# Row tests moved into the experts' hand-set order, one chunk's bonus sums moved ahead of its scores, and the verdict read before the last expert

## The chip, the cores and the metric

The kernel runs on one core of one Trainium2 chip. A core has five engines with an instruction queue each: TensorE (PE in the profile, with its weight loads as PEld), VectorE (DVE), ScalarE (ACT), GpSimd (POOL) and SyncE (SP, which here issues most DMA transfers). They wait for each other by semaphores alone. The metric is device time in microseconds (us). The kernel before took 307.76 us, the median of three runs (306.99, 307.76, 310.99).

## The reference, cut to what matters

The first half is a gated linear attention with a state of 48 x 48 for each of 4 x 8 heads over 768 steps; the second sends each token with a positive skip score to one of eight experts.

```python
for t in range(S):                       # S = 768, state: B, H, 48, 48
    cur = einsum('bhd,bhe->bhde', u * k[t], v[t])
    y[t] = einsum('bhd,bhde->bhe', r[t], state + cur)
    state = w[t][..., None] * state + einsum('bhd,bhe->bhde', k[t], v[t])
x = y as (3072 tokens, 384)
do_compute = x @ w_skip > 0
xc = x[do_compute]
logits = xc @ w_gate                     # 8 experts
gate_w = softmax(logits) of the chosen expert, e_idx = argmax(logits)
for e in range(8):
    y[e_idx == e] = gate_w * (relu(xc @ w1[e]) @ w2[e])
out[do_compute] = xc + y
```

## The kernel before, in words

The attention is done in 24 chunks of 128 steps, six for each of four batches, all eight heads at once. A chunk's decays are cumulated by two scans on DVE (L266 gives `q`, L288 gives `rh`), POOL makes the scaled keys `kq` (L283), the scaled reads `rp` (L293) and the products `rk` for the bonus term (L275). On PE a chunk is: transposed keys (L305), scores of keys against reads (L312, into the two banks psA), bonus sums (L327, psB), the rows of the chunk before (L378, psX), the state's update (L341, psu), and the outputs (L362 and L367, psY). DVE masks the scores (L318) and writes the bonus into psY (L331); the outputs of the chunk add to that, so L362 needs both masks and L331. ACT does the copies out of PSUM.

The order of this part is written out by hand: a loop over `s` (L574 to L650) emits, at step `s`, the outputs of chunk `s`, the scores of chunk `s + 1` and the scans of chunk `s + 2`, and every engine keeps the order in which its instructions were written. `drip` mixes steps of the router in, which ranks tokens within their expert (L390 to L507). Behind the loop a second hand-ordered block (L668 to L689) runs the first half of expert 0 while the last group of six chunks is routed, and a third (L824 to L827) runs the experts; in that one POOL has its place by hand too, SP has not.

The experts work in products of split numbers: each weight and token matrix is a high and a low part, and three products are added. Expert `e` does eight groups of hidden columns (psH, L780 to L782), ACT and DVE split them into `hh` and `hl`, then two groups of 128 tokens (`j` = 0, 1) go through the second layer (psO, L804 to L806), DVE forms `fin` (L811), and POOL scatters it to the output by an indirect DMA (L744). Between these, ACT and DVE split the next expert's weights (L89, L90: `w1l`, `w2l`).

The kernel also tests whether its short cuts held: on DVE, L696 to L707 test rows of `ends`, `lows`, `gall` and `rall` and leave sums in `vt`; PE adds these over the partitions (L710, L711, psf), and DVE writes the verdict `flag_i` (L712). These lines stand outside the hand-ordered blocks, so that a scheduler chose their places. At the end of the program `values_load` (L834) reads `flag_i` into a register of each of the five engines, and a branch on it (L835) runs the slow general path if a test failed. It does not for these inputs.

Of the kernel before, what the change touches and what calls it, by code (L numbers as in the profile page):

```python
# [8 lines left out]
F32 = mybir.dt.float32  # L9
# [6 lines left out]
ALU = mybir.AluOpType  # L16
# [40 lines left out]
def rwkv_moe_kernel(ctx, tc, wrk, wrk0, vN, uP, wgs, wgp, w12, cst, out):  # L57
# [64 lines left out]
    with tc.tile_pool(name="att", bufs=2) as att, \  # L122
# [173 lines left out]
            nc.scalar.copy(ends[:, i], work[i].pop("rh")[:, :, P])  # L296
            nc.scalar.copy(lows[:, i], work[i]["q"][:, :, 0])

        def intra(i):
            b, c = seq[i]  # L300
            wk = work[i]
            if c < NC - 1:
                pst = ps1.tile([P, NP, P], F32, tag="psT", name=f"psT{i}", bufs=2)
                for a in range(NP):
                    nc.tensor.transpose(pst[:, a], wk["kq"][:, a], ident)  # L305
                kt = wk["kt"] = att.tile([P, NP, P], F32, tag="kt", name=f"kt{i}")
                nc.scalar.copy(kt, pst)
            for a in range(NP):
                for j in (0, HP):
                    for g in range(2):  # L310
                        rows = slice(64 * g, 64 * g + HP)
                        nc.tensor.matmul(psa[g][j:j + HP, a, j:], wk["kq"][rows, a, j:j + HP],  # L312
                                         wk["rp"][rows, a, j:], start=True, stop=True)
# [9 lines left out]
        def bonus_sums(i):  # L323
            wk = work[i]
            wk["psb"] = ps1.tile([P, NP, P], F32, tag="psB", name=f"psB{i}")
            for a in range(NP):
                nc.tensor.matmul(wk["psb"][:, a], ubk_sb[:, a], wk["rk"][:, a],  # L327
                                 start=True, stop=True)
# [242 lines left out]
        with tc.manual_schedule():  # L571
            setup()
            fill(FILL0)
            for s in range(-2, n + 1):  # L574
# [40 lines left out]
                if on(s):  # L615
                    evict(s)
                if on(s + 1):
                    intra(s + 1)
                    drip(2 * pace[0])
                    mask(s + 1, 0)  # L620
                    mask(s + 1, 1)
                    drip(pace[0])
                    bonus_sums(s + 1)
                    bonus(s + 1)
                if s == -1:
                    prep_reads(1)
# [41 lines left out]
        with tc.manual_schedule(engines={nc.tensor.engine, nc.scalar.engine, nc.vector.engine}):  # L668
# [17 lines left out]
            for k in range(done[0], 6 * FC - 4):  # L686
# [1 line left out]
            early_tokens(1)  # L688
            drain(todo)  # L689


        vt = keep.tile([P, 5], F32, name="vt")
        good = keep.tile([P, n * NP], F32, name="good")
        good_ = keep.tile([P, n * NP], F32, name="good_")
        ends_ = ends.rearrange("p c a -> p (c a)")
        nc.vector.tensor_scalar(good_, ends_, 1.0 - TOL, None, op0=ALU.is_ge)  # L696
        nc.vector.scalar_tensor_tensor(good, ends_, 1.0 + TOL, good_, op0=ALU.is_le, op1=ALU.mult)
        nc.vector.scalar_tensor_tensor(good, lows.rearrange("p c a -> p (c a)"), Q_MIN, good,
                                       op0=ALU.is_ge, op1=ALU.mult)
        nc.vector.tensor_reduce(vt[:, 0:1], good, axis=AX, op=ALU.add)  # L700
        nc.vector.tensor_scalar(vt[:, 0:1], vt[:, 0:1], n * NP - 0.5, None, op0=ALU.is_le)
        fine = good[:, :B * NC]
        nc.vector.tensor_scalar(fine, gall[:, :, 0], 0.1, None, op0=ALU.is_ge)
        nc.vector.tensor_reduce(vt[:, 1:2], fine, axis=AX, op=ALU.add)
        nc.vector.tensor_reduce(vt[:, 2:3], rall[:, :, 0], axis=AX, op=ALU.max)
        nc.vector.tensor_scalar(vt[:, 2:3], vt[:, 2:3], float(CAP), None, op0=ALU.is_ge)
        nc.vector.scalar_tensor_tensor(vt[:, 3:4], vt[:, 1:2], B * NC - 0.5, vt[:, 2:3],  # L707
                                       op0=ALU.is_le, op1=ALU.add)
        psf = ps1.tile([P, 512], F32, tag="psT", name="psf", bufs=2)
        nc.tensor.matmul(psf[0:1, 0:1], rowsk, vt[:, 0:1], start=True, stop=False)  # L710
        nc.tensor.matmul(psf[0:1, 0:1], rows1_, vt[:, 3:4], start=False, stop=True)  # L711
        nc.vector.tensor_scalar(flag_i, psf[0:1, 0:1], 0.0, None, op0=ALU.is_gt)  # L712


    with tc.tile_pool(name="wset1", bufs=1) as ws1, tc.tile_pool(name="moe", bufs=2) as moe:
        wset1[0] = ws1
        def pair(e, instr=None):
# [8 lines left out]
        pair(1)  # L726
        pair(2)
        later_pairs = list(range(3, E))
        first = []

        xTs = {}
# [11 lines left out]
        def scatter(s, o):  # L743
            sc = nc.gpsimd.indirect_dma_start(  # L744
                out=out, out_offset=bass.IndirectOffsetOnAxis(ap=ids[:, s % 2, s // 2:s // 2 + 1],
                                                               axis=0),
                in_=o, in_offset=None, bounds_check=NT - 1, oob_is_err=False)
            tc.declare_no_dep(sc.ins, group="rows", reason="tokens are scattered to rows of their own")
            tc.add_to_no_dep_group("rows", sc.ins)

        def expert(e):
            todo = []
# [47 lines left out]
            for j in range(1 if e == 0 else 0, 2):  # L800
                pso = ps1.tile([P, DM], F32, tag=("psu", "pss")[j], name=f"psO{e}_{j}")
                for fc in range(FC):
# [3 lines left out]
                    nc.tensor.matmul(pso, h[j, fc][1], w2h[:, o], start=False,  # L806
                                     stop=(fc == FC - 1))
                more(2)
                s = 2 * e + j
                o = moe.tile([P, DM], F32, tag="fin", name=f"fin{e}_{j}", bufs=3)  # L810
                nc.vector.scalar_tensor_tensor(o, pso, gates[:, j, e:e + 1], xg[s],  # L811
# [4 lines left out]
                    scatter(s, o)  # L816
                if s == 2 * E - 3:
                    nc.gpsimd.drain()
            more(12)
            if e + 2 < E:  # L820
                drain(load_weights(e + 2, 0))
# [9 lines left out]

    rv = nc.values_load(flag_i[0:1, 0:1], min_val=0, max_val=2)  # L834
    with tc.If(rv > 0):  # L835
        general_path(tc, wrk, w12, yd, uP, c_sb, wgs_sb, out)

# [155 lines left out]
```

## Time and profile before

| | |
|---|---|
| median of 3 runs | 307.76 us |
| the profiled execution's own time | 307.14 us |
| span of its trace, first to last instruction | 305.4 us |
| PE busy | 290.0 us (95%) |
| DVE busy | 216.8 us (71%) |
| ACT, POOL busy | 175.4 us (57%), 141.2 us (46%) |
| mean granted TensorE clock | 0.997 |

A time line of an engine has the start in us from the span's start, the length, the engine, the line of the kernel, the operation and its tiles, and in brackets the idle time ahead of it with what ended it. DVE and PE overlap the end of one instruction with the start of the next, so that the distance between starts can be smaller than a length. A letter q behind an engine's name (DVEq) marks its sequencer, which takes instructions ahead of the engine.

### The profile page before, as it was taken

How to read it: one execution, taken by the hardware profiler on the slowest of the kernel's cores; microseconds unless marked ns; L12 is line 12 of the kernel's file. 1: busy time of each engine (PE TensorE's matmuls, PEld its weight loads, DVE VectorE, ACT ScalarE, POOL GpSimd, SP SyncE). 2: the span in 40 equal slices, each digit the busy share in tenths (PEclk: the TensorE clock that was granted, in tenths of full speed). 3: DMA queues.
4: the chain of work that ended last, by engine and by line, in shares of the span. 5: the costliest groups of instructions: out<-in, count | busy, mean ns of one | idle time of the engine just before them, and what ended most of it. 6: DMA issues, size and time to landing. Idle time of an engine off the chain costs nothing.

```text
span 305.4 us, 8275 instructions
## 1 busy us (share of the span) xinstructions
PE 290.0 (95%) x3228; PEld 269.3 (88%) x3228; DVE 216.8 (71%) x410; ACT 175.4 (57%) x493; POOL 141.2 (46%) x140
## 2 busy tenths in 40 slices
PE   6799999999999999897999999999999999999991
PEld 2689888888889988786888999999999999999991
DVE  6887779868888778977263868594958859495310
ACT  5365736799577976796232656391837648182300
POOL 7886565977966598775106662402011010201111
PEclk9999999999999999999999999999999999999998
DMA  7999999998799988836323699846265564610000
GB/s 193 270 255 260 293 258 246 227 256 217 206 294 282 266 185 206 252 124 217 116 76 86 171 368 342 296 166 245 90 239 204 206 248 146 245 70 26 9 21 22
DMA packets 22738, 60.29 MB, mean 197 GB/s; under 512 B 3926, under 2 KB 10490, under 8 KB 22688
## 3 DMA queue, kind: packets, MB, share of 16 engines
q1 hardware_dynamic: 20176, 53.79, 60.6%
q0 software_dynamic: 2048, 5.48, 5.7%
q8 instruction: 27, 0.44, 0.7%
q10 hardware_dynamic: 464, 0.40, 0.6%
q14 instruction: 23, 0.19, 0.2%
HBM read 52.60 MB, written 7.86 MB: 198 GB/s over the span
## 4 chain that ended last, share of the span: by engine, by line
PE 60%; DVE 4%; DMA 4%; issue 0%; ACT 0%; POOL 0%; POOLq 0%; SPq 0%; DVEq 0%
PE psO L806 7%; PE psO L804 7%; PE psO L805 7%; PE psH L782 7%; PE psH L781 7%; PE psH L780 7%; DMA vt<-wrk 3%; PE psY L362 3%; PE psY L367 3%; PE psB L327 3%; PE psA L312 2%; PE psH L115 2%; PE psX L378 2%; PE psX L739 2%; DVE psY L331 1%; PE psO L561 1%
## 5 line engine op out<-in xcount | busy, mean ns | idle before, releaser
L744 POOL DMA_INDIRECT out<-fin,ids x16 | 16.7, 1044 | 99.4 <-DVE fin L811 93.3
L787 ACT ACTIVATE hh<-psH 128x256 fp32r<-128x256 f32 x60 | 23.0, 384 | 57.1 <-PE psH L782 53.3
L782 PE MATMUL psH<-xTh,w1l 128*128 128x256 f32 x168 | 47.5, 283 | 0.0
L781 PE MATMUL psH<-xTl,w1h 128*128 128x256 f32 x168 | 47.5, 283 | 0.0
L780 PE MATMUL psH<-xTh,w1h 128*128 128x256 f32 x168 | 47.5, 283 | 0.0
L318 DVE TENSOR_TENSOR asb<-psA,c_sb 128x512 f32<-128x512 f32 x48 | 30.8, 683 | 16.8 <-PE psA L312 16.8
L804 PE MATMUL psO<-w2h,hh 128*128 128x384 f32 x120 | 40.8, 340 | 0.0
L806 PE MATMUL psO<-w2h,hl 128*128 128x384 f32 x120 | 40.2, 335 | 0.0
L805 PE MATMUL psO<-w2l,hh 128*128 128x384 f32 x120 | 40.1, 334 | 0.0
L275 POOL TENSOR_TENSOR rk<-wrk 128x512 f32<-128x512 f32 x24 | 31.3, 1305 | 5.8 <-POOL rp L293 2.2
L792 DVE SCALAR_TENSOR_TENSOR hl<-psH,hh 128x256 fp32r<-128x256 f32 x60 | 25.2, 419 | 11.8 <-ACT hh L787 10.0
L288 DVE TENSOR_TENSOR_SCAN rh<-wrk,pss 128x520 f32<-128x520 f32 x24 | 29.6, 1235 | 4.2 <-PE pss L495 2.4
L782 PEld LDWEIGHTS psH<-xTh,w1l 128*128 128x128 f32 x168 | 32.2, 192 | 0.0
L781 PEld LDWEIGHTS psH<-xTl,w1h 128*128 128x128 f32 x168 | 32.2, 192 | 0.0
L780 PEld LDWEIGHTS psH<-xTh,w1h 128*128 128x128 f32 x168 | 32.2, 191 | 0.0
L283 POOL TENSOR_TENSOR kq<-wrk,q 128x512 f32<-128x512 f32 x24 | 28.3, 1178 | 7.7 <-DVE q L266 6.5
L293 POOL TENSOR_TENSOR rp<-wrk,rh 128x512 f32<-128x512 f32 x23 | 27.1, 1180 | 8.9 <-DVE rh L288 7.2
L811 DVE SCALAR_TENSOR_TENSOR fin<-psO,gates,xg 128x384 f32<-128x384 f32 x15 | 9.3, 618 | 30.3 <-PE psO L806 27.1
L266 DVE TENSOR_TENSOR_SCAN q<-wrk,pss 128x520 f32<-128x520 f32 x24 | 29.3, 1222 | 1.7 <-DMA wrk<-wrk 1.4
L362 PE MATMUL psY<-asb,v 128*48 128x128 f32 x384 | 26.6, 276 | 3.5 <-DVE short L514 2.0
L90 DVE TENSOR_TENSOR w2l<-r,w2h 128x512 fp32r<-128x512 f32 x42 | 27.9, 689 | 0.8
L89 ACT CAST w2h<-r 128x512 fp32r<-128x512 f32 x48 | 27.9, 626 | 0.6 <-DMA r<-w 0.6
(148 smaller groups left out, 653.0 us busy)
## 6 DMA issues: line engine op xcount, KB each, us to landing
r<-w SPq DMA_DIRECT2D x48, 512.0 KB, 5.6
wrk<-wrk SPq DMA_DIRECT2D x23, 579.4 KB, 7.8
v<-vN SPq DMA_DIRECT2D x24, 192.0 KB, 6.0
out<-x SPq DMA_DIRECT2D x24, 192.0 KB, 2.5
vt<-wrk SPq DMA_DIRECT2D x46, 96.0 KB, 7.1
wrk<-wrk SPq DMA_DIRECT2D x1, 384.0 KB, 4.5
vt<-wrk ACTq DMA_DIRECT2D x1, 256.0 KB
out<-fin,ids POOLq DMA_INDIRECT x16
```

The costliest lines, as they stand in the source:

```text
L266: nc.vector.tensor_tensor_scan(q.rearrange("p a j -> p (a j)")[:, ::-1], t[:, 1:1 + n_][:, ::-1], ones_at[:, 1:1 + n_][:, ::-1], 0.0, op0= ...
L275: nc.gpsimd.tensor_tensor(work[i]["rk"].rearrange("p a j -> p (a j)"), t[:, R_OFF:K_OFF], t[:, K_OFF:V_OFF], op=ALU.mult)
L283: nc.gpsimd.tensor_tensor(kq, wk["k"], wk["q"][:, :, 1:1 + P], op=ALU.mult)
L288: nc.vector.tensor_tensor_scan(rh.rearrange("p a j -> p (a j)"), wk["w"][:, 0:NP * CW], ones_at[:, :NP * CW], 1.0, op0=ALU.mult, op1=ALU.max)
L318: nc.vector.tensor_tensor(s, psa[g], tri.rearrange("p (o j) -> p o j", o=1).to_broadcast([P, NP, P]), op=ALU.mult)
L362: nc.tensor.matmul(psy[64 * g:64 * g + D, a], v[:, 2 * a + g], wk["asb"][g][:, a], start=False, stop=(c == 0), skip_group_check=True)
L780: nc.tensor.matmul(ps, w1h[:, o:o + P], xTh[:, kc], start=(kc == 0), stop=False)
L781: nc.tensor.matmul(ps, w1h[:, o:o + P], xTl[:, kc], start=False, stop=False)
L782: nc.tensor.matmul(ps, w1l[:, o:o + P], xTh[:, kc], start=False, stop=(kc == KC - 1))
L804: nc.tensor.matmul(pso, h[j, fc][0], w2h[:, o], start=(fc == 0), stop=False)
L805: nc.tensor.matmul(pso, h[j, fc][0], w2l[:, o], start=False, stop=False)
L806: nc.tensor.matmul(pso, h[j, fc][1], w2h[:, o], start=False, stop=(fc == FC - 1))
```

## The change

It does three things. For the chunk 1 alone (the second), the four bonus sums stand ahead of the scores on PE. The row tests become a function that expert 1 calls behind its first group of 128 tokens, and PE's two sums and the verdict another one that expert 2 calls at the same place. And `values_load` stands in expert 6, behind its second group, instead of at the end; the branch stays at the end.

```diff
-        def intra(i):
+        def rows_of_keys(i):
...
                 nc.scalar.copy(kt, pst)
+
+        def scores(i):
+            wk = work[i]
             for a in range(NP):
...
                 if on(s + 1):
-                    intra(s + 1)
+                    rows_of_keys(s + 1)
+                    if s == 0:
+                        bonus_sums(1)
+                    scores(s + 1)
                     drip(2 * pace[0])
                     mask(s + 1, 0)
                     mask(s + 1, 1)
                     drip(pace[0])
-                    bonus_sums(s + 1)
+                    if s != 0:
+                        bonus_sums(s + 1)
                     bonus(s + 1)
...
+        def row_tests():
+            ends_ = ends.rearrange("p c a -> p (c a)")
+            nc.vector.tensor_scalar(good_, ends_, 1.0 - TOL, None, op0=ALU.is_ge)
...
+            nc.vector.scalar_tensor_tensor(vt[:, 3:4], vt[:, 1:2], B * NC - 0.5, vt[:, 2:3],
+                                           op0=ALU.is_le, op1=ALU.add)
+
+        def verdict():
+            psf = ps1.tile([P, 512], F32, tag="psT", name="psf", bufs=2)
+            nc.tensor.matmul(psf[0:1, 0:1], rowsk, vt[:, 0:1], start=True, stop=False)
+            nc.tensor.matmul(psf[0:1, 0:1], rows1_, vt[:, 3:4], start=False, stop=True)
+            nc.vector.tensor_scalar(flag_i, psf[0:1, 0:1], 0.0, None, op0=ALU.is_gt)
...
                 more(2)
+                if j == 0 and e in (1, 2):
+                    (row_tests, verdict)[e - 1]()
                 s = 2 * e + j
...
                 if s == 2 * E - 3:
                     nc.gpsimd.drain()
+                    verdicts.append(nc.values_load(flag_i[0:1, 0:1], min_val=0, max_val=2))
...
-    rv = nc.values_load(flag_i[0:1, 0:1], min_val=0, max_val=2)
+    rv = verdicts[0]
     with tc.If(rv > 0):
```

The ten instructions of the tests are the same ten as before (L696 to L707). What moved is best seen in the engines' orders.

DVE, in the attention, behind the last scan of chunk 23 (`rh`), before: `good`, `vt` are the row tests, `asb_22` the masked scores of chunk 22, psY its bonus, `short` a step of the router.

```order
L288 SCALAR_TENSOR_TENSOR rh_2315<-wrk_85,pss 128x520
L696 TENSOR_SCALAR good__2615<-ends 128x96
L697 SCALAR_TENSOR_TENSOR good<-ends,good__2615 128x96
L698 SCALAR_TENSOR_TENSOR good<-lows,good 128x96
L700 TENSOR_REDUCE vt<-good 128x1
L701 TENSOR_SCALAR vt<-vt 128x1
L318 TENSOR_TENSOR asb_22_2344<-psA_108,c_sb 128x512
L318 TENSOR_TENSOR asb_22_2346<-psA_109,c_sb 128x512
L331 TENSOR_TENSOR psY<-psB_2348,vt_88 128x512
L514 TENSOR_SCALAR short<-psC 1x1
```

The same place now:

```order
L288 SCALAR_TENSOR_TENSOR rh_2315<-wrk_85,pss 128x520
L321 TENSOR_TENSOR asb_22_2344<-psA_108,c_sb 128x512
L321 TENSOR_TENSOR asb_22_2346<-psA_109,c_sb 128x512
L334 TENSOR_TENSOR psY<-psB_2348,vt_88 128x512
L517 TENSOR_SCALAR short<-psC 1x1
```

Five row tests stood between the scan and the masks; now the masks follow the scan. The other five, which stood among the last group's router steps, are gone from there too, and all ten stand in expert 1 between the fourth of the second-layer weight splits after the hidden groups and `fin_0`.

PE, in chunk 1, from its last scores on, before (psA are scores, psB the bonus sums, psX the rows of chunk 0, psu the state):

```order
L312 MATMUL psA_108<-rp_236,kq_199 64x64
L312 MATMUL psA_109<-rp_236,kq_199 64x64
L327 MATMUL psB_307<-rk_196,ubk_sb 128x128 x4
L378 MATMUL psX_315<-wgp_sb,xT_278 128x105 x4
L341 MATMUL psu<-v_169,kt_285 64x48
L341 MATMUL psu<-v_169,kt_285 48x48
```

PE in chunk 1 now, from its transposed keys (psT) on:

```order
L305 MATMUL psT_280<-c_sb,kq_199 128x128 x4
L330 MATMUL psB_287<-rk_196,ubk_sb 128x128 x4
L315 MATMUL psA_108<-rp_236,kq_199 64x128
L315 MATMUL psA_109<-rp_236,kq_199 64x128
L315 MATMUL psA_108<-rp_236,kq_199 64x64
```

The bonus sums went past the sixteen score products, and psX now follows the scores.

DVE at the end of the program, before (TENSOR_LOAD is the read of the verdict, `g_r` belongs to the general path):

```order
L792 SCALAR_TENSOR_TENSOR hl_7_4234<-psH_7_4232,hh_7_4233 128x256
L811 SCALAR_TENSOR_TENSOR fin_0_4271<-psO_0_4246,gates,xg_2826 128x384
L811 SCALAR_TENSOR_TENSOR fin_1_4301<-psO_1_4276,gates,xg_2830 128x384
L834 TENSOR_LOAD flag_i
L835 COMPARE_AND_BRANCH
```

DVE now, at the end of expert 6 and at the end of the program:

```order
L823 SCALAR_TENSOR_TENSOR fin_1_4128<-psO_1_4099,gates,xg_2790 128x384
L831 TENSOR_LOAD flag_i
L802 SCALAR_TENSOR_TENSOR hl_0_4150<-psH_0_4148,hh_0_4149 128x256
...
L823 SCALAR_TENSOR_TENSOR fin_0_4285<-psO_0_4260,gates,xg_2812 128x384
L823 SCALAR_TENSOR_TENSOR fin_1_4315<-psO_1_4290,gates,xg_2816 128x384
L848 COMPARE_AND_BRANCH
```

The read went ahead of expert 7's work on DVE, and likewise on PE, ACT and POOL. On SP, where the scheduler chooses, it went from ahead of expert 2's weight loads to between the two halves of expert 4's.

## Rows read from the trace of the kernel before

**Rows 1.** Busy time per engine in the experts' stretch (us busy, instructions in brackets)

```profile
168.00:299.00 131.00, 131.00 (x938) 130.76 (x936) 87.89 (x166) 67.61 (x152) 26.88 (x26) 1.00 0.52 181
```

**Rows 2.** Time line of PE, 138 to 145 us

```profile
138.94 1.09 PE L312 MATMUL psA<-rp,kq 64*64 64x128 f32 x32
...
142.52 0.16 PE L512 MATMUL psC<-ohs,onesb 128*1 128x1 bf16 x1
144.65 1.08 PE L362 MATMUL psY<-asb,v 128*48 128x128 f32 x16 [1.97 <-DVE short L514]
```

**Rows 3.** Time line of DVE, 140 to 145 us

```profile
140.25 0.37 DVE L696 TENSOR_SCALAR good__2615<-ends 128x96 f32<-128x96 f32 x1 [0.45 <-ACT ends L296]
140.65 1.30 DVE L697 SCALAR_TENSOR_TENSOR good<-ends,good__2615 128x96 f32<-128x96 f32 x1
142.06 0.26 DVE L698 SCALAR_TENSOR_TENSOR good<-lows,good 128x96 f32<-128x96 f32 x1
...
142.71 1.28 DVE L318 TENSOR_TENSOR asb<-psA,c_sb 128x512 f32<-128x512 f32 x2
143.91 0.69 DVE L331 TENSOR_TENSOR psY<-psB,vt 128x512 f32<-128x512 f32 x1
```

**Rows 4.** Time line of POOL beside it

```profile
140.67 1.17 POOL L293 TENSOR_TENSOR rp<-wrk,rh 128x512 f32<-128x512 f32 x1
```

**Rows 5.** Time line of PE, chunk 1

```profile
14.64 1.09 PE L312 MATMUL psA<-rp,kq 64*64 64x128 f32 x32 [0.72 <-POOL rp L293]
...
18.23 1.08 PE L362 MATMUL psY<-asb,v 128*48 128x128 f32 x16
```

**Rows 6.** Time line of DVE, chunk 1

```profile
16.31 1.26 DVE L318 TENSOR_TENSOR asb<-psA,c_sb 128x512 f32<-128x512 f32 x2
17.49 0.69 DVE L331 TENSOR_TENSOR psY<-psB,vt 128x512 f32<-128x512 f32 x1
```

**Rows 7.** Time line of DVE, the last group's router

```profile
157.35 0.18 DVE L703 TENSOR_SCALAR good<-gall 128x24 f32<-128x24 f32 x1
157.44 0.20 DVE L448 TENSOR_REDUCE rall<-rnk 128x6 f32<-128x48 f32 x1
```

**Rows 8.** Time line of DVE, second layer of expert 1, start of expert 2

```profile
189.85 0.62 DVE L811 SCALAR_TENSOR_TENSOR fin<-psO,gates,xg 128x384 f32<-128x384 f32 x1 [0.81 <-PE psO L806]
190.38 1.35 DVE L90 TENSOR_TENSOR w2l<-r,w2h 128x512 fp32r<-128x512 f32 x2
194.01 0.62 DVE L811 SCALAR_TENSOR_TENSOR fin<-psO,gates,xg 128x384 f32<-128x384 f32 x1 [2.28 <-PE psO L806]
195.49 0.42 DVE L792 SCALAR_TENSOR_TENSOR hl<-psH,hh 128x256 fp32r<-128x256 f32 x1 [0.86 <-ACT hh L787]
```

**Rows 9.** Costliest groups on the page: weight splits on DVE (us in all, mean ns)

```profile
L90 DVE TENSOR_TENSOR w2l<-r,w2h 128x512 fp32r<-128x512 f32 x42 | 27.9, 689 | 0.8
```

**Rows 10.** Reads of the verdict, by line (ns min/median/max, start us)

```profile
L834 PEldq TENSOR_LOAD <-flag_i x1: 487/487/487, 295.8 to 295.8; - x1
L834 DVEq TENSOR_LOAD <-flag_i x1: 537/537/537, 299.1 to 299.1; - x1
```

**Rows 11.** The branch behind the read on DVE, by line

```profile
L835 DVEq COMPARE_BRANCH  x1: 72/72/72, 300.1 to 300.1; - x1
...
L835 DVEq EVENT_SEMAPHORE  x1: 21/21/21, 304.2 to 304.2; - x1
```

**Rows 12.** Time line of POOL, scatters behind experts 6 and 7

```profile
283.06 0.98 POOL L744 DMA_INDIRECT out<-fin,ids  x1 [2.97 <-DVE fin L811]
...
300.01 0.98 POOL L744 DMA_INDIRECT out<-fin,ids  x1 [3.18 <-DVE fin L811]
```

**Rows 13.** Busy time per stretch; the last two columns are DMA share, GB/s

```profile
285.00:285.50 0.50, 0.50 (x6) 0.50 (x6) 0.15 (x1) 0.11 (x1) 0.00 (x0) 1.00 0.00 0
...
303.00:303.50 0.50, 0.00 (x0) 0.00 (x0) 0.00 (x0) 0.00 (x0) 0.00 (x0) 1.00 0.02 3
```

**Rows 14.** DMA queues, 300.7 to 301.5 us: packets, MB, share of 16 engines

```profile
q14 instruction: 3, 0.02, 16.1%
q8 instruction: 1, 0.02, 8.6%
```

More of the change, by code (lines that the diff above doesn't have):

```diff
@@ L689, in rwkv_moe_kernel @@
             drain(todo)
[L692 to L712, printed above, removed]
     with tc.tile_pool(name="wset1", bufs=1) as ws1, tc.tile_pool(name="moe", bufs=2) as moe:
@@ L728, in rwkv_moe_kernel @@
         later_pairs = list(range(3, E))
+        verdicts = []
         first = []
@@ L749, in scatter @@
             tc.add_to_no_dep_group("rows", sc.ins)
+        vt = keep.tile([P, 5], F32, name="vt")
+        good = keep.tile([P, n * NP], F32, name="good")
+        good_ = keep.tile([P, n * NP], F32, name="good_")
+        def row_tests():
+            ends_ = ends.rearrange("p c a -> p (c a)")
+            nc.vector.tensor_scalar(good_, ends_, 1.0 - TOL, None, op0=ALU.is_ge)
+            nc.vector.scalar_tensor_tensor(good, ends_, 1.0 + TOL, good_, op0=ALU.is_le, op1=ALU.mult)
+            nc.vector.scalar_tensor_tensor(good, lows.rearrange("p c a -> p (c a)"), Q_MIN, good,
+                                           op0=ALU.is_ge, op1=ALU.mult)
+            nc.vector.tensor_reduce(vt[:, 0:1], good, axis=AX, op=ALU.add)
+            nc.vector.tensor_scalar(vt[:, 0:1], vt[:, 0:1], n * NP - 0.5, None, op0=ALU.is_le)
+            fine = good[:, :B * NC]
+            nc.vector.tensor_scalar(fine, gall[:, :, 0], 0.1, None, op0=ALU.is_ge)
+            nc.vector.tensor_reduce(vt[:, 1:2], fine, axis=AX, op=ALU.add)
+            nc.vector.tensor_reduce(vt[:, 2:3], rall[:, :, 0], axis=AX, op=ALU.max)
+            nc.vector.tensor_scalar(vt[:, 2:3], vt[:, 2:3], float(CAP), None, op0=ALU.is_ge)
+            nc.vector.scalar_tensor_tensor(vt[:, 3:4], vt[:, 1:2], B * NC - 0.5, vt[:, 2:3],
[5 more added lines that the diff above has]
+            nc.vector.tensor_scalar(flag_i, psf[0:1, 0:1], 0.0, None, op0=ALU.is_gt)
         def expert(e):
```

## The prediction, made before the result was known

> **What bounds the kernel now.** I read the page first, then the busy time by stretch, then PE's time line, then DVE's beside it, and the last six us by line. The reader is to see three things.
>
> From 168 to 299 us PE is busy 131.00 of 131.00 us [rows 1]: in the experts nothing but PE sets the time, and whatever the other engines do there costs nothing as long as PE is not made to wait. What PE saves ahead of 168 us therefore reaches the end undiminished, unless a later wait eats it.
>
> In the attention PE is near full too, with one large hole. At 144.65 PE starts L362 after 1.97 us of idleness, its last work before that being L512 at 142.52 [rows 2]. The row names "short" as what ended it. But L362 reads the masked scores and the bonus in psY, and the bonus, L331, ended at 143.91 + 0.69 = 144.60 [rows 3], 0.05 us before PE moved. So L331 is what PE waited for.
>
> Behind PE's last product, near 299.1 us, come `fin`, the scatter and the branch, and the span ends at 305.4. These six us have no PE work in them.
>
> **The change part by part.**
>
> *Five tests out of the attention.* DVE was free from 140.25 - 0.45 = 139.80 [rows 3], and the scores of chunk 22 were done at 138.94 + 1.09 = 140.03 [rows 2]. The masks L318 started only at 142.71, because five row tests, issued from 140.25 on, stood ahead of them [rows 3]. Without them the masks start near 140.1, or 2.6 us earlier, and L331 ends near 142.0. PE reaches L362 at about 142.65, when L512 is through. L331 is then no longer late, PE's own queue is, and the gain is the whole hole: 144.65 - 142.65 = 2.0 us. What follows on PE up to the experts hangs on products of its own, or on steps of the router and the first gather that start from the same masks and move with them. The bounds: 1.97 us of idle time and no more; nothing, if another input of L362 were late at the same instant. I take 2.0.
>
> One thing in these rows bears on the new place. L697 took 1.30 us and L698, on as many elements, 0.26 [rows 3]; L697 ran from 140.65 to 141.95 and POOL's `rp` from 140.67 to 141.84 [rows 4].
>
> *Five tests out of the router.* L703 started at 157.35 and the router's next step at 157.44 [rows 7], so a test of this kind holds the chain back by at most 0.09 us by starts, and that only if the step behind it was ready. Five times that is 0.45 at most. I take 0, because those steps wait for each other anyway, and keep 0.45 for the range.
>
> *Ten tests into expert 1.* In the second layer DVE stood idle for 0.81 us before the first `fin`, 2.28 before the second and 0.86 before the first `hl` of expert 2 [rows 8], or 3.95 together. The first five tests took 142.71 - 140.25 = 2.46 with L697 at 1.30; at 0.26 they take 1.4. The second five, at 0.18 to 0.20 each like L703, take 1.0 [rows 3, 7]. So 2.4 us, or 3.5 with L697 slow; both lie inside 3.95. Queued behind them are `fin`, two `w2l` splits and with these the next load of weights on SP, which comes up to 3.5 - 0.81 = 2.7 us later. PE reads that expert's weights only one expert on, so this is covered: 0. If the cover were gone, the excess over 3.95 would reach `hl` and then PE.
>
> *PE's two sums into expert 2.* They leave PE's queue in front of expert 0 and enter it between two groups of expert 2, with the same two one-column products: 0. The verdict on DVE is one tiny instruction ahead of a `fin`.
>
> *Chunk 1.* PE waited 0.72 us for POOL's `rp` before the scores [rows 5]. Now it does the bonus sums in that time. That is the upper bound of the gain. But L362 of this chunk started at 18.23, and DVE's L331, which it needs, ended at 17.49 + 0.69 = 18.18; DVE had been busy without a break since the masks at 16.31 [rows 5, 6]. The sums can start at 14.64 - 0.72 = 13.92; if they take about as long as the scores, 1.1 us, the scores end near 16.1, still ahead of 16.31. So DVE keeps its times, PE waits for L331 instead of for `rp`, and the gain is 0.
>
> *The read of the verdict into expert 6.* A read takes 0.49 us on PE's sequencer. There it stood at 295.8 while PE worked on to 299 [rows 1, 10], so the sequencer was 3 us ahead and a read of half a us inside the stream is covered: 0. On SP the next load waits for a split that comes behind the verdict anyway: 0.
>
> *The tail.* On DVE the read began at 299.1 and the branch at 300.1; only 4.1 us after the branch, at 304.2, did DVE go on [rows 10, 11]. Without the read the branch can start 1.0 us earlier. The Trainium skill ("Runtime: NRT & Kernel Launch", section on instruction fetch mechanics) says that a taken branch out of the loaded window must fetch its target by DMA before it goes on; by that rule the fetch stays and merely starts earlier, so that the tail would give the same 1.0. The trace agrees as far as it shows four instruction packets right then [rows 14]. But the end also waits for the last scatter. It was issued at 300.01 and its traffic was still there after 303.0, 3 us later; the scatter issued at 283.06 had no traffic left at 285.0 [rows 12, 13]. The fetches fall between the two and may be what slows it. If so they leave its way as they move; if not, the scatter keeps the end where it is. Bounds: 0 and 1.0. The branch began 0.4 us after the read was over (299.1 + 0.54 against 300.1), so something besides the read holds it; that speaks for the lower half, and I take 0.4.
>
> **The sum.** 2.0 + 0.4 = 2.4 us. The profiled execution took 307.14, so it would become 304.7; the median of the runs, 307.76, lies 0.6 above it, which makes 305.4. I put the forecast between the two, at **305.0**.
>
> **The rivals.**
>
> *More is gained.* The tail gives its full 1.0 (0.6 more), and the router's 0.45 comes on top: 305.0 - 1.05, about 303.9. For it: each fetch that leaves the scatter's way. Against it: several things end within half a us of each other at 304.2, and all must move. Chance 0.14.
>
> *The hole stays.* The masks move forward, and PE waits at the next place instead: for the first gather, for ACT's copy, or for a weight load of expert 0. Then the 2.0 are given back, and with the tail at 0 to 0.4 the time is 307.0 to 307.5. For it: the chain behind the hole runs through DVE, POOL and a DMA before PE meets it. Against: that chain starts from the same DVE instructions, which move 1.8 us or more. Or the tests were not what held the masks, and the change does not do what it says; rows 3 leave little room for that. Chance 0.16.
>
> *Slower: the tests collide with POOL in expert 1.* The one test that ran wholly beside a POOL instruction took 1.30 us [rows 3, 4]. POOL issues gathers and scatters during expert 1 too. If all ten tests took 1.30 there, that is 13.0 us against 3.95 of idle time [rows 8]: the first `hl` of expert 2 would be 9.05 us late, PE with it, and the time 307.14 - 2.4 + 9.05, near 313.8. It costs more than it saves once the tests take over 3.95 + 2.4 = 6.4 us together. Against it: two weight splits beside such a scatter took 1.35 [rows 8], 0.68 each, and their mean is 0.689 [rows 9], so POOL's indirect transfers do not slow DVE. The Trainium skill ("SBUF — State Buffer", section on SBUF's two separate sides) has a lock that would do it: a DVE instruction with two inputs from SBUF and a GpSimd instruction that reads SBUF exclude each other for the whole instruction. Rows 3 and 4 fit it; by it alone three of the ten tests could be held for a POOL instruction each. Chance 0.04.
>
> The forecast itself has 0.64; its own range, from the unknown tail, the router and the gap of 0.6 between profile and median, is 304.0 to 306.0. A remaining 0.02 is for what I don't see.
>
> **Range and chances.** 303.2 to 306.4 holds the forecast and the case with more gained, and leaves out the hole that stays and the slower one, 0.2. Two per cent, about what a measurement of this kernel can tell from no change, is 6.2 us. No case but the slower one comes near it: faster 0.02, within 0.96, slower 0.02.
>
> **What would show it.** In the changed kernel's trace DVE's masks of chunk 22 follow the scan of chunk 23 by less than 0.5 us, and PE's L362 there shows no idle time above 0.2; if 1.97 is there again, or as much at one of the next three waits, the first step is wrong. In chunk 1 the wait for `rp` is gone and about 0.5 stands at L362; if PE starts L362 before 18.0, that term was mis-sized. In expert 1 the ten tests take 2.4 to 3.5 us and PE has no gap; a gap there is the third rival. At the end the branch on DVE follows `fin` at once. The step from the last product to the span's end, 6.3 us now, should be 5.3 to 6.3. The forecast fails if PE has a new gap anywhere in the experts, most of all where the verdict is read behind expert 6.

## The result, and the profile after

The changed kernel took 304.62 us, the median of 4 runs (303.77 to 306.77); the forecast was 305.0, with a range of 303.2 to 306.4. The kernel before has 309.38 beside it (306.99 to 312.03, 4 runs): the three runs known already and one more, at 312.03. The ratio is 0.985 with a 95% interval of 0.980 to 0.990: faster by 1.5%, within the 2% that the forecast named. Run twice more, on two chips, it gave 304.86 (ratio 0.987, 0.982 to 0.992) and 304.62 (0.984, 0.979 to 0.988). Medians here are of all runs of a set, while the ratios leave out runs over 1.5% above the fastest of their kernel.

The profiled execution took 304.25 us with a span of 302.5. Between the two traces the difference is 305.35 - 302.46 = 2.89 us, and it lies in four places: the start came 0.44 later (L362 of chunk 1 at 18.23, now 18.67), the hole at chunk 22 is 2.04 shorter, from chunk 23 to the last `fin` 0.05 was saved, and the end is 1.24 shorter.

**The hole.** PE's time line of the changed kernel, same columns as [rows 2]; L365 is the former L362:

```profile
139.37 1.09 PE L315 MATMUL psA<-rp,kq 64*64 64x128 f32 x32
...
142.95 0.16 PE L515 MATMUL psC<-ohs,onesb 128*1 128x1 bf16 x1
143.04 1.08 PE L365 MATMUL psY<-asb,v 128*48 128x128 f32 x16
```

And DVE's beside it, to be held against [rows 3]:

```profile
139.00 1.24 DVE L288 TENSOR_TENSOR_SCAN rh<-wrk,pss 128x520 f32<-128x520 f32 x1 [1.29 <-PE pss L498]
140.53 1.29 DVE L321 TENSOR_TENSOR asb<-psA,c_sb 128x512 f32<-128x512 f32 x2 [0.29 <-PE psA L315]
141.73 0.69 DVE L334 TENSOR_TENSOR psY<-psB,vt 128x512 f32<-128x512 f32 x1
```

The masks now wait 0.29 us for their scores instead of standing behind five tests, L334 ends at 142.42, and PE goes from L515 to L365 without a gap.

**Expert 1.** DVE's time line, with the ten tests where [rows 8] had idle time:

```profile
186.63 0.20 DVE L741 TENSOR_SCALAR good__2639<-ends 128x96 f32<-128x96 f32 x1
186.86 0.26 DVE L742 SCALAR_TENSOR_TENSOR good<-ends,good__2639 128x96 f32<-128x96 f32 x1
187.16 0.26 DVE L743 SCALAR_TENSOR_TENSOR good<-lows,good 128x96 f32<-128x96 f32 x1
...
188.49 0.16 DVE L752 SCALAR_TENSOR_TENSOR vt<-vt 128x1 f32<-128x1 f32 x1
188.58 0.62 DVE L823 SCALAR_TENSOR_TENSOR fin<-psO,gates,xg 128x384 f32<-128x384 f32 x1
189.12 1.28 DVE L90 TENSOR_TENSOR w2l<-r,w2h 128x512 fp32r<-128x512 f32 x2
191.96 0.62 DVE L823 SCALAR_TENSOR_TENSOR fin<-psO,gates,xg 128x384 f32<-128x384 f32 x1 [1.55 <-PE psO L816]
193.44 0.42 DVE L802 SCALAR_TENSOR_TENSOR hl<-psH,hh 128x256 fp32r<-128x256 f32 x1 [0.87 <-ACT hh L797]
```

From 186.63 to 188.65 they take 2.0 us in all; the idle time before the first `fin` is used up, 1.55 and 0.87 are left before the next `fin` and `hl`, and PE in the experts has none, as [rows 1] before:

```profile
168.00:297.00 129.00, 129.00 (x923) 128.72 (x922) 88.46 (x174) 66.67 (x148) 26.44 (x25) 1.00 0.51 182
```

**Chunk 1.** PE, then DVE, to be held against [rows 5, 6]:

```profile
14.58 1.06 PE L330 MATMUL psB<-rk,ubk_sb 128*128 128x128 f32 x8
15.57 1.09 PE L315 MATMUL psA<-rp,kq 64*64 64x128 f32 x32
16.91 1.14 PE L381 MATMUL psX<-wgp_sb,xT 128*128 128x105 f32 x8 [0.26 <-ACT xT L375]
17.98 0.67 PE L344 MATMUL psu<-v,kt 128*64 128x48 f32 x16
18.67 1.08 PE L365 MATMUL psY<-asb,v 128*48 128x128 f32 x16
```

```profile
16.74 1.27 DVE L321 TENSOR_TENSOR asb<-psA,c_sb 128x512 f32<-128x512 f32 x2
17.93 0.69 DVE L334 TENSOR_TENSOR psY<-psB,vt 128x512 f32<-128x512 f32 x1
```

The wait for `rp` is gone. L365 starts 0.05 us after DVE's L334 ended (18.62), and PE's own queue is through at the same instant.

**The end.** The reads of the verdict by line, then the branch on DVE (in answer to [rows 10, 11]), then the last scatter on POOL [rows 12]:

```profile
L831 PEldq TENSOR_LOAD <-flag_i x1: 487/487/487, 277.2 to 277.2; - x1
L831 DVEq TENSOR_LOAD <-flag_i x1: 542/542/542, 280.5 to 280.5; - x1
```

```profile
L848 DVEq COMPARE_BRANCH  x1: 72/72/72, 297.5 to 297.5; - x1
...
L848 DVEq EVENT_SEMAPHORE  x1: 21/21/21, 300.9 to 300.9; - x1
```

```profile
298.36 0.98 POOL L728 DMA_INDIRECT out<-fin,ids  x1 [3.18 <-DVE fin L823]
```

The branch starts with `fin` (297.47) and not 1.0 us behind the read's start. From the end of PE's last product (297.43) to the span's end it is 5.0 us now, against 6.3 before. What ran on the DMA queues during the scatter's traffic, before from 301.2 to 303.4 us and then after from 299.6 to 300.6 (packets, MB, share of 16 engines):

```profile
q0 software_dynamic: 64, 0.04, 11.2%
q14 instruction: 2, 0.02, 4.5%
```

```profile
q0 software_dynamic: 64, 0.04, 15.7%
```

Before, instruction packets travel with the scatter's 64 packets; after, they are through by then, and the scatter has the engines to itself.

### The profile page after: what moved, and what is told of

Its sections match the earlier page's. It is cut to its first block, busy times and chain, and to the rows that moved or that the text cites. A ratio compares the mean times of both kernels' runs of the same rounds, so it can differ in the third digit from the quotient of the medians.

```text
span 302.5 us, 8272 instructions
## 1 busy us (share of the span) xinstructions
PE 289.8 (96%) x3228; PEld 269.3 (89%) x3228; DVE 216.8 (72%) x410; ACT 176.2 (58%) x493; POOL 141.3 (47%) x140
## 4 chain that ended last, share of the span: by engine, by line
issue 32%; PE 23%; DVE 5%; POOL 5%; DMA 4%; ACT 1%; POOLq 1%; SPq 0%; DVEq 0%
POOL out L728 5%; PE psY L370 3%; PE psY L365 3%; PE psB L330 3%; PE psA L315 3%; PE psX L381 2%; PE psH L115 2%; DMA vt<-wrk 2%; DMA v<-vN 1%; PE psu L344 1%; DMA xg<-out,idr 1%; DVE psY L334 1%; PE psH L792 1%; PE psH L791 1%; PE psH L790 1%
## 5 line engine op out<-in xcount | busy, mean ns | idle before, releaser
L90 DVE TENSOR_TENSOR w2l<-r,w2h 128x512 fp32r<-128x512 f32 x42 | 27.8, 687 | 1.0
L365 PE MATMUL psY<-asb,v 128*48 128x128 f32 x384 | 26.6, 276 | 1.8 <-DVE psY L334 1.3
L89 ACT CAST w2h<-r 128x512 fp32r<-128x512 f32 x48 | 27.9, 626 | 0.4 <-DMA r<-w 0.4
L330 PE MATMUL psB<-rk,ubk_sb 128*128 128x128 f32 x192 | 27.7, 287 | 0.0
```

What stands on the lines that cost most here:

```text
L365: nc.tensor.matmul(psy[64 * g:64 * g + D, a], v[:, 2 * a + g], wk["asb"][g][:, a], start=False, stop=(c == 0), skip_group_check=True)
```

## The experiments

Three intervals of the traces carry the reading, all from starts on the time lines: from the first product of L362 in chunk 21 to that in chunk 22, from there to chunk 23, and from the last `fin` to the span's end; beside them the median and the ratio to the kernel before.

| kernel | 21 to 22 | 22 to 23 | fin to end | median us | ratio (95%) |
|---|---|---|---|---|---|
| before, first trace | 8.70 | 5.20 | 6.23 | | |
| before, second trace | 8.70 | 6.61 | 6.27 | 310.67 | 1.003 (0.999 to 1.007) |
| tests alone | 6.66 | 5.20 | 5.87 | 305.45 | 0.986 (0.978 to 0.994) |
| read alone | 8.71 | 6.81 | 4.98 | 308.03 | 0.994 (0.990 to 0.997) |
| bonus alone | 8.70 | 6.81 | 5.86 | 307.57 | 0.989 (0.981 to 0.998) |
| bonus alone, again | 8.70 | 6.81 | 5.62 | 309.26 | 0.999 (0.995 to 1.003) |
| hole filled | 8.70 | 5.20 | 5.91 | 309.68 | 0.998 (0.994 to 1.002) |
| changed | 6.66 | 5.20 | 4.99 | 304.62 | 0.985 (0.980 to 0.990) |
| changed, again | 6.66 | 5.21 | 4.99 | 304.86 | 0.987 (0.982 to 0.992) |
| changed, third | 6.66 | 5.20 | 4.97 | 304.62 | 0.984 (0.979 to 0.988) |
| changed, no branch | 6.66 | 5.20 | 4.70 | 305.48 | 0.983 (0.976 to 0.989) |

The medians do not follow these intervals closely. Against the kernel before, the tests alone gained 4.8 us where the expectation has 1.7 to 2.1, the read alone 2.2 instead of 1.2, and the kernel without a branch 4.8 instead of 2.9 to 3.2; on one chip the tests alone and the kernel without a branch come out alike, though their ends differ by 1.17. The times also hold the start of the program, where L362 of chunk 1 comes at 18.2 to 22.8 us, and stretches at half the clock. What a part is worth is therefore read from the intervals.

**The tests alone.** Against the changed kernel:

```diff
-                    if s == 0:
-                        bonus_sums(1)
...
-                    if s != 0:
-                        bonus_sums(s + 1)
+                    bonus_sums(s + 1)
...
-                    verdicts.append(nc.values_load(flag_i[0:1, 0:1], min_val=0, max_val=2))
...
-    rv = verdicts[0]
+    rv = nc.values_load(flag_i[0:1, 0:1], min_val=0, max_val=2)
```

> Only the ten row tests and PE's two sums are moved (experts 1 and 2); chunk 1 has its old order and the verdict is read at the program's end. Theory: the hole of 1.97 us ahead of L362 of chunk 22 was the tests', and nothing behind it gives it back: no idle time above 0.2 there, PE's products behind 168 us start some 2.0 to 2.4 us earlier than before, against the products ahead of chunk 22; the end, from the last fin's start to the span's end, is 6.2 us as before. In all 1.7 to 2.1 us faster than the kernel before. Rival (the hole comes back at the gather or in expert 1): 0 to 0.5 us faster.

The hole is gone and did not come back: 6.66, and 149.44 us from chunk 23 to the last `fin`, against 149.27 in the first trace of before. The end stayed long at 5.87, though not quite as long as 6.23.

**The read alone.** Against the kernel before:

```diff
                 if s == 2 * E - 3:
                     nc.gpsimd.drain()
+                    verdicts.append(nc.values_load(flag_i[0:1, 0:1], min_val=0, max_val=2))
...
-    rv = nc.values_load(flag_i[0:1, 0:1], min_val=0, max_val=2)
+    rv = verdicts[0]
```

> Only the read of the verdict is moved into expert 6; the tests stay where the scheduler put them and chunk 1 keeps its order. Theory: the fetches behind the branch start earlier and leave the last scatter's way. The hole of about 2.0 us at chunk 22 stays; from the last fin's start to the span's end 5.0 us instead of 6.2, the scatter's last packet lands about 2.1 us after its issue instead of 3.3: 1.2 us faster than the kernel before. Rival (the scatter's 3.3 us were chance, the read itself counts for nothing): from fin to the end 5.8 to 6.2 us and 0 to 0.4 us faster.

The end is 4.98, 1.25 shorter than in the first trace of before, with the hole still there: the theory's 1.2. The scatter's way from issue to landing is the last column of these rows on the DMA issues, of the second trace of before, of the tests alone, of the read alone and of the kernel without a branch:

```profile
out<-fin,ids POOLq DMA_INDIRECT x1, 3.8
```

```profile
out<-fin,ids POOLq DMA_INDIRECT x1, 3.4
```

```profile
out<-fin,ids POOLq DMA_INDIRECT x1, 2.6
```

```profile
out<-fin,ids POOLq DMA_INDIRECT x1, 2.2
```

It is 3.2 to 3.8 us in the four traces with a late read that give it (3.2 in bonus alone, again), 2.6 or 2.7 in four with an early one (2.6 in the changed kernel too), and 2.2 where nothing is fetched at all. In each of these nine traces the span ends 1.4 to 1.6 us after this landing, as it should if the scatter is what the end waits for.

**No branch.** The changed kernel without the last lines:

```diff
-    rv = verdicts[0]
-    with tc.If(rv > 0):
-        general_path(tc, wrk, w12, yd, uP, c_sb, wgs_sb, out)
```

> The changed kernel without the branch and the general path behind it (so the fallback for inputs that fail the row tests is left out); the tests and PE's sums stay. It shows what ends the program when nothing is fetched. Theory: in the changed kernel the last scatter already sets the end, not the branch: from the last fin's start to the span's end 4.7 to 5.0 us against 4.96, the scatter's last packet again about 2.1 us after its issue; 2.9 to 3.2 us faster than the kernel before. Rival (the branch's fetch still sets the end): 4.5 us or less, 3.4 us or more faster than the kernel before.

The end is 4.70, at the theory's lower edge and 0.29 below the changed kernel's. So by the first trace of before the early read has taken out 1.24 of the 1.53 us that read and branch cost at the end (6.23 - 4.70). Single ends vary: 5.62 to 6.27 in the six traces that read late, 4.88 to 5.15 in the seven that read early, which makes 1.0 on average.

**Chunk 1's order alone, twice.**

```diff
-                    intra(s + 1)
+                    rows_of_keys(s + 1)
+                    if s == 0:
+                        bonus_sums(1)
+                    scores(s + 1)
```

> Only chunk 1's bonus sums stand ahead of its scores. Theory: DVE's bonus write is the last input of L362 of chunk 1 either way, so the wait of PE moves from rp to that write and nothing is gained: 0 us, the hole at chunk 22 and the 6.2 us at the end as before. Rival (the wait for rp was lost time): 0.7 us faster, the distance from the first scores of chunk 0 to L362 of chunk 1 shorter by as much.

> Chunk 1's bonus sums alone, again, with more executions. Theory as revised: L362 of chunk 1 follows that of chunk 0 by 5.6 us instead of 5.8 to 6.0, so 0.2 to 0.4 us faster than the kernel before at an equal clock. Rival 1 (nothing, as forecast): 0.0. Rival 2 (what its four first runs gave): 1.5 to 2.0 us faster.

The first ratio, 0.989, looked like a gain of three us; twelve more runs took it back to 0.999. In the traces L362 of chunk 1 follows that of chunk 0 by 5.59 and 5.81 us; with the old order it was 5.98 and 6.14 (before, the second with the granted clock at 0.50 in that stretch), 5.77 (tests alone, read alone, hole filled). A gain near 0.2 us fits, and the times can't show it.

**The kernel before again.**

> The kernel before once more, unchanged. It shows how far executions of one kernel lie apart and what the hole at chunk 22 costs from one to the next. Theory (the hole has a second price): in the runs of the kernel before on this chip, 308.0 to 308.8 us go with a mean granted clock of 0.997 to 0.998 and 309.6 to 312.1 with 0.982 to 0.992; most executions show the granted clock at 0.50 for some 3 us right behind the hole, and so more than the 305.4 us of span that the first trace shows, some 1.6 us more each time. If this profile shows the fall, PE's products behind 148 us lie 1.5 to 1.7 us later against the ones ahead of 144 us than in the first trace. Rival (the spread comes from the start alone): the distance from L362 of chunk 1 to the last product is the same in both traces, and only the time up to L362 of chunk 1 differs.

The fall is there. The windows of that trace around its hole (PE, PEld, DVE, ACT, POOL busy, granted clock, DMA share, GB/s):

```profile
145.00:146.00 1.00, 0.00 (x0) 0.00 (x0) 1.00 (x3) 0.90 (x4) 0.00 (x0) 1.00 0.43 163
146.00:147.00 1.00, 0.10 (x2) 0.10 (x4) 0.90 (x4) 0.77 (x3) 0.00 (x0) 0.76 0.93 230
147.00:148.00 1.00, 1.00 (x11) 0.99 (x12) 0.29 (x3) 0.00 (x0) 0.49 (x1) 0.50 0.83 279
148.00:149.00 1.00, 1.00 (x9) 0.64 (x6) 0.00 (x0) 0.00 (x0) 0.73 (x1) 0.50 0.30 119
149.00:150.00 1.00, 1.00 (x6) 1.00 (x7) 0.00 (x0) 0.00 (x0) 0.00 (x0) 0.53 0.48 114
150.00:151.00 1.00, 1.00 (x29) 0.88 (x31) 0.00 (x0) 0.48 (x1) 0.00 (x0) 1.00 0.21 83
```

PE's time line there, to be held against the last row of [rows 2]:

```profile
146.90 1.95 PE L362 MATMUL psY<-asb,v 128*48 128x128 f32 x16 [1.98 <-DVE short L514]
148.78 1.70 PE L367 MATMUL psY<-rp,sblk 128*128 128x128 f32 x8
150.41 1.09 PE L312 MATMUL psA<-rp,kq 64*64 64x128 f32 x32
```

Behind 1.98 us of idle time the granted clock stands at 0.50, the lower of its two levels (1.2 GHz), for some three us: the same products of L362 take 1.95 instead of 1.08, and chunk 23 comes 6.61 - 5.20 = 1.41 us later, a little under the 1.5 to 1.7 expected. Of the five traces with this hole left idle four show it, at a price of 1.4 to 1.6 us; the first trace of before, from which the forecast was worked out, is the one that doesn't. The rival has the larger part in this trace: of the 3.59 us between the two spans the start makes 2.21 (L362 of chunk 1 at 20.44 here against 18.23), with a fall of its own from 13 to 17 us, behind 1.74 us of waiting for `v` of the first chunk.

**The hole filled.** The kernel before, with PE busy in its hole:

```diff
+                if s == n - 2:
+                    fill(8)
                 if on(s):
                     outputs(s)
```

> The kernel before, with eight products of 128x512 on a constant tile (0.21 us each, no result used) put ahead of the outputs of chunk 22 on PE, where PE stands idle for 1.97 us. The hole stays as long, but PE works in it. Theory (the fall of the granted clock comes from the idle hole): the distance from L362 of chunk 21 to that of chunk 22 stays 8.70 us, the distance from there to chunk 23 is 5.20 us and not 6.6 to 6.8, no stretch near 147 us with a granted clock of 0.50, and the median lies 1 to 1.5 us under that of the kernel before. Rival (the fall has nothing to do with the idle time): 6.6 to 6.8 us from chunk 22 to 23 again, 0 us.

PE's time line (one of the eight records is missing):

```profile
142.89 0.16 PE L512 MATMUL psC<-ohs,onesb 128*1 128x1 bf16 x1
143.03 1.89 PE L569 MATMUL psw<-warm 128*128 128x512 bf16 x7
145.03 1.08 PE L362 MATMUL psY<-asb,v 128*48 128x128 f32 x16
```

No fall, and 5.20 to chunk 23: as the theory has it, in the one trace there is. By itself this trace would not settle it, since the first trace of before has the hole idle and no fall either. But none of the eight traces of kernels without the hole has a fall there, and four of the five with the hole idle have one. The time is not as expected: 0.998, no gain. In that execution PE stood idle elsewhere, in expert 1 (PE, then ACT, then DVE):

```profile
185.09 0.28 PE L783 MATMUL psH<-xTl,w1h 128*128 128x256 f32 x1 [0.82 <-issue]
...
186.05 0.39 PE L782 MATMUL psH<-xTh,w1h 128*128 128x256 f32 x1 [0.57 <-DVE hl L794]
```

```profile
185.16 0.38 ACT L789 ACTIVATE hh<-psH 128x256 fp32r<-128x256 f32 x1 [1.99 <-remote]
```

```profile
185.57 0.42 DVE L794 SCALAR_TENSOR_TENSOR hl<-psH,hh 128x256 fp32r<-128x256 f32 x1 [1.68 <-ACT hh L789]
```

The windows there, with the same columns as above:

```profile
182.00:184.00 2.00, 2.00 (x18) 1.83 (x16) 1.12 (x2) 0.89 (x2) 1.70 (x2) 1.00 1.01 406
184.00:186.00 2.00, 0.66 (x5) 0.43 (x3) 0.42 (x1) 0.84 (x3) 0.09 (x1) 1.00 1.05 381
186.00:188.00 2.00, 1.95 (x10) 1.95 (x11) 1.92 (x5) 2.00 (x7) 0.00 (x0) 0.59 0.62 203
```

The DMA engines are full and DVE is busy for 0.42 of 2 us. PE waits first 0.82 us with no cause shown and then 0.57 for DVE's `hl`, `hl` waited 1.68 for ACT's `hh`, and `hh` 1.99 for something that the profile can't name ("remote"). The weight splits (L89, L90) have no idle time ahead of them in this stretch, so that a late load of weights is not shown; and in the first trace of the changed kernel the DMA engines are as full from 176 to 184 us (1.02 to 1.05) while PE is busy throughout. What held PE here stays open. The clock falls there in its turn. From chunk 23 to the last `fin` it took 152.87 us instead of 149.27.

**The first five tests one place further on.** The changed kernel, with the five in the attention again, but behind the bonus of chunk 22:

```diff
+                if s == n - 2:
+                    scan_tests()
                 if on(s + 1):
                     rows_of_keys(s + 1)
```

> The changed kernel with its first five row tests back in the attention, one place behind the old one: behind the bonus of chunk 22 on DVE, ahead of the masks of chunk 23, where DVE stands idle from 143.7 to 146.3 us. Theory (the price of the tests was their place ahead of the masks, not the attention): L362 of chunk 22 follows that of chunk 21 by 6.66 us and chunk 23 by 5.20 more, as in the changed kernel; 0.0 us against it. Rival (a test that meets POOL's work takes 1.3 us there again, and the masks of chunk 23 come late): chunk 23 up to 0.9 us later.

The first half holds: 6.66 to chunk 22, and L581 (the former L697) took 0.26 us. To chunk 23 it was 5.49 and not 5.20. There the masks start at 147.70, while PE's scores had ended at 147.35 (rows of DVE, then PE):

```profile
144.82 0.26 DVE L581 SCALAR_TENSOR_TENSOR good<-ends,good__118 128x96 f32<-128x96 f32 x1
...
147.70 1.29 DVE L321 TENSOR_TENSOR asb<-psA,c_sb 128x512 f32<-128x512 f32 x2 [1.66 <-PE psA L315]
```

```profile
146.26 1.09 PE L315 MATMUL psA<-rp,kq 64*64 64x128 f32 x32
```

POOL issued a gather from 146.27 to 147.49 that the five tests had made later by standing ahead of its address; whether that held the masks stays open. The kernel's time, 309.16 (ratio 0.990, 0.985 to 0.996), tells little of the tests: in the trace PE stands idle in expert 1 for 0.78 and 1.99 us, as in the kernel with the filled hole, which ran on the same chip. Its three runs with a mean clock of 0.997 or more took 304.49 to 306.37, like the changed kernel.

**The scan of chunk 2 later.**

```diff
-                    if s != -1:
+                    if s not in (-1, 0):
                         prep_reads(s + 2)
...
-                if s == -1:
-                    prep_reads(1)
+                if s in (-1, 0):
+                    prep_reads(s + 2)
```

> The changed kernel with the scan of chunk 2 (rh, 1.23 us) behind the masks and the bonus of chunk 1 on DVE, instead of ahead of them. Theory (DVE's bonus write is what L362 of chunk 1 waits for, which is why the order of PE's sums gained little there): L362 of chunk 1 follows that of chunk 0 by 0.2 to 0.5 us less than 5.60, and the scores of chunk 2 are not late; 0.2 to 0.5 us faster than the changed kernel. Rival (PE's own queue sets L362 of chunk 1, or the reads of chunk 2 come late by as much): 0 to 0.5 us slower.

Chunk 1 follows chunk 0 by 5.60 us, as in the changed kernel; the time is 306.91 (0.991, 0.987 to 0.994). The masks then wait 0.77 for their scores, and L334 (17.49 + 0.69 = 18.18) is followed by L365 at 18.24, right behind PE's own L344 again. So in the new order DVE and PE's queue end together there, and taking one away gains nothing: the rival's side, at its end of 0.

**Two more moves that looked free.**

```diff
-                    drip(2 * pace[0])
+                    if s != LATE:
+                        drip(2 * pace[0])
                     mask(s + 1, 0)
...
                 flush()
+                if s == LATE:
+                    drip(3 * pace[0])
...
                 tokens(e + 1)
+            if e == 2:
+                verdict()
```

> The changed kernel with two more moves. The router's steps of step 18 go behind the masks and the bonus of chunk 19 on DVE, and the rank sums on PE behind the outputs of chunk 19; there PE waits 0.90 us for L334. PE's two sums of the verdict go next to the transposes of expert 2 instead of between two groups of products. Theory: two instructions of 0.20 us each leave the way of the masks, so the idle time at L365 of chunk 19 shrinks from 0.90 to 0.5, and the sums cost 0.2 instead of 0.37: 0.4 to 0.6 us faster than the changed kernel. Rival (the wait moves to the rank sums or to the next masks): 0.

Neither was: 308.85 (0.999, 0.996 to 1.002). PE's time line at chunks 19 and 20, and in expert 2:

```profile
128.07 1.08 PE L365 MATMUL psY<-asb,v 128*48 128x128 f32 x16 [0.58 <-DVE psY L334]
135.10 1.08 PE L365 MATMUL psY<-asb,v 128*48 128x128 f32 x16 [0.63 <-DVE psY L334]
...
207.31 0.19 PE L761 MATMUL psf<-vt,rowsk 128*1 128x1 f32 x2 [1.52 <-DVE xTl L90]
```

Chunk 19 gains 0.32, chunk 20 waits 0.63 where it didn't, and the sums, which need a bank that the split `xTl` must first have read, wait 1.52. A further 3.7 us of its profile lie in the start (L362 of chunk 1 at 22.79 against 19.09 in the changed kernel on the same chip), with a fall of the clock from 13 to 20 us behind 2.01 us of waiting for `v`; why most of its runs show mean clocks near 0.99 was not settled.

**The changed kernel again, twice.**

> The changed kernel, unchanged, on the same chip as the kernel before. Theory: no hole at chunk 22, so no fall of the granted clock behind it, and mean clocks of 0.995 or more in most runs; the difference to the kernel before is 2.0 (hole) + 1.2 (end) + 0.2 (chunk 1) where neither shows a fall, 3.0 to 3.5 us, and 4.5 to 5 us by the medians, because most executions of the kernel before have the fall. Rival (the fall of the clock comes at random and hits both alike): 3.0 us by the medians too, clocks of 0.992 and less as often as in the kernel before.

> The changed kernel, unchanged, once more. In the two traces of before with tests and products put elsewhere in the attention (taken on one chip), PE stood idle in expert 1, behind weight splits that waited for their loads while the DMA engines were full, and the granted clock fell there. Theory (this is a matter of how fast the loads run in an execution, and the changed kernel is open to it as the others are): the same products, with 6.66 us from chunk 21 to 22 and 5.20 on to 23; and from chunk 23 to the last fin either 149.2 to 149.5 us, or, where the loads run late, 152 us and more with idle time at PE's hidden layer of expert 1; 3 to 5 us faster than the kernel before by the medians. Rival (the place of the tests in expert 1 protects from it): 149.2 to 149.5 always and a spread of the runs under 2 us.

On the one chip its mean clocks were 0.997 to 0.999 in five runs of six; of the 29 runs of the kernel before beside it, 11 were at 0.997 or more and 18 at 0.993 or less. The 11 have a median of 308.34 us, the changed kernel's five one of 304.85: 3.5 us at equal clocks. All runs together differ by 309.50 - 304.86 = 4.6. The falls therefore do not hit both alike. Two cautions belong to this. In every trace the clock also falls behind PE's last product, where it costs PE nothing, and this is in the mean: the first trace of the changed kernel has 0.995 with no fall before it. And kernels without the hole are not safe from falls elsewhere: two more moves had a mean clock of 0.994 or less in 10 of 12 runs, the first five tests one place further on in 7 of 10. In the third trace 149.46 us passed from chunk 23 to the last `fin`, and the runs spread by 1.9 us; no idle time of PE in expert 1 was seen in any of the changed kernel's three traces, so whether it is open to that stays open, and the expectation's rival was not refuted. The third trace has a fall of its own, in the start, behind 1.85 us of waiting for `v` of the first chunk. That weight splits waited for their loads in the two traces with idle time in expert 1, as the expectation has it, their rows don't show.

## Why the prediction was right, point by point

*Tests out of the attention, 2.0:* right, 2.04 in every trace with the tests moved, and nothing behind gave it back.

*Tests out of the router, 0 (bound 0.45), and PE's two sums, 0:* small, as taken. Between the two first traces PE's waits for `sg` and for the gather shrank by 0.06 and 0.16, the removed sums gave 0.23 ahead of expert 0, and in expert 2 they cost 0.37. From chunk 23 to the last `fin` the three traces of the changed kernel have 149.22 to 149.46, those of before 149.15 and 149.27.

*Tests into expert 1, 0:* right, at 2.0 us in all, less than the 2.4 to 3.5 forecast. The slow test was the point on which the third rival hung. The former L697 took 1.30 or 1.31 us in all six traces in which it stood beside POOL's product `rp` [rows 3, 4], and 0.26 in the eight in which it stood elsewhere. L743, which has two inputs as well, began at 187.16, just ahead of the scatter that POOL issued from 187.24, and took 0.26; in the third trace of the changed kernel it ran at 190.83, inside a scatter from 190.78 to 191.78, and took 0.26 again. By the Trainium skill ("SBUF — State Buffer", section on SBUF's two separate sides) a DVE instruction with two inputs from SBUF and a GpSimd instruction that reads SBUF exclude each other for the whole instruction; of the rows here L697 beside `rp` fits that, and L743 inside the scatter shows no such hold.

*Chunk 1, 0:* near enough, 0.2 by the traces and nothing by the times. The idle time of about 0.5 at L362 that was to show it is not there. The wait did not move to DVE's write alone, as the prediction had it, but to DVE's write and PE's queue at once.

*The read in mid-stream, 0:* right; PE has no gap behind expert 6.

*The end, 0.4: this is the step that was mis-sized.* It is 1.24 in the changed kernel and 1.25 with the read alone against the trace that the forecast started from, above the upper bound of 1.0 too; over all traces it is 1.0, at that bound. The step from the last product to the span's end, 5.0 us, lies outside the 5.3 to 6.3 that the prediction named as a sign. The prediction weighed two ways, that the branch merely starts earlier (1.0) or that the scatter holds the end (0), and took the lower half because the branch had begun 0.4 after the read was over. That time went with the read: now the branch follows `fin` at once. And the scatter is slower with the fetches beside it; the prediction named this ("the fetches fall between the two and may be what slows it") and gave it no price beyond the earlier start. The way from issue to landing is 2.6 instead of 3.2 to 3.8. The Trainium skill's rule on a branch out of the loaded window ("Runtime: NRT & Kernel Launch", instruction fetch mechanics) agrees with the trace as far as it goes: the fetch stayed (DVE goes on at 300.9, 3.4 us behind its branch) and moved. What it does to a transfer beside it only the runs showed.

*What the sum lacked* is the second price of the hole, 1.4 to 1.6 us of half clock behind it in most executions of before. It is part of why the medians differ by near 5 us and not by the forecast's 2.8: at equal clocks it was 3.5, by all runs of that set 4.6. How much of the rest is the hole's, and how much belongs to falls elsewhere, is not shown; filling the hole gained nothing in 12 runs. The forecast time was right all the same because the profiled execution of before had no fall, nor have most of the changed kernel's: 307.14 less what the traces lost, 2.89, is the profiled 304.25. There is luck in this too, for the 0.84 us that the end gave beyond the forecast met 0.44 by which the start came later. The median of three that stood beside it, 307.76, was low; in the four later sets of runs the kernel before had medians of 309.5 to 310.3. Its third run, 310.99, was the sign: 3.9 us above a profile in which nothing explains such a spread.

## What to carry to other kernels

Work without a deadline on an engine that keeps its order costs what it holds up: the same five tests cost 2.0 us ahead of the masks and nothing in expert 1's idle time. Price a hole on PE from more than one execution, by the runs' granted clocks as well as by the idle time in the one trace, since the products behind it may run at half speed. And let a branch whose target must be fetched know its verdict early, so that the fetch is over before the last transfer that the end waits for.

## What the runs showed of the hardware

PE's idle time of 1.97 to 1.98 us was followed by some three us at a granted clock of 0.50 in four traces of five; 0.90 us at chunk 19 was followed by none in any trace that has it. In the start, 1.74, 1.85 and 2.01 us of waiting were (second trace of before, third of the changed kernel, two more moves) and 1.68 was not (second of the changed kernel). A scatter of 64 packets took 2.2 us from issue to landing alone, 2.6 with instruction packets just ahead of it and 3.2 to 3.8 with them beside it. A test with two inputs took 1.3 us beside a product on POOL and 0.26 inside a scatter. In two executions PE stood idle in expert 1, for a cause that the rows leave open; with the fall of the clock that followed it cost 3.6 us in the one (152.87 - 149.27).
